# An attention and feed-forward kernel: the first feed-forward product of the last three token groups as seven block products, two of them with softplus in one pass, and another order from the middle on

## The chip, the core and the metric

The kernel runs on one core of a Trainium2 chip. Its time is the device time of one execution in microseconds (us); the three runs shown below are taken of the kernel as it stands before the change. The engines are TensorE (PE, matmuls; PEld is its weight load), VectorE (DVE), ScalarE (ACT), GpSimd (POOL), and SyncE (SP), whose queue issues nearly all transfers. Each engine works through its own list of instructions strictly in order and waits for the others by semaphores.

## What is computed

The attention output of 4 sequences of 768 tokens, 8 heads of 64 channels, is the input of a feed-forward layer with softplus between its two products:

```python
scores = scale * np.matmul(q, k.transpose(0, 1, 3, 2))      # 4 x 8 x 768 x 768
keep   = is_global | is_local                               # 8 global keys, 96 local ones
bias   = -slopes[:, None, None] * dist[None, :, :]
a      = softmax(where(keep, scores + bias, -1e9))
x      = matmul(a, v).transpose(0, 2, 1, 3).reshape(3072, 512)
h      = x @ w_in                                           # 3072 x 512 by 512 x 2048
g      = np.maximum(h, 0.0) + np.log1p(np.exp(-np.abs(h)))  # softplus
out    = g @ w_out                                          # 3072 x 2048 by 2048 x 512
```

## The kernel before

**Tiles.** The 3072 tokens are 24 blocks of 128 (numbered n in the order in which they are attended), two blocks make a unit of loading (i, 12 of them), and two make a token group (g, 12 of them, 256 tokens) for the feed-forward layer. Weights and activations are bf16 in SBUF; products accumulate in fp32 in PSUM.

**The order is written out by hand.** Every piece of work is an operation with a name, an engine and the tiles that it reads and writes (`Program.op`, L28). The string `ORDER` (L68) lists all names with a letter for the engine (P is PE, V is DVE, A is ACT, G is POOL, S is SP); `in_order` (L56) issues them in just this order, so each engine's list is the sequence of its own letters in the string. Waits follow from the tiles: a PSUM bank that is written again waits for whoever still reads it. Where an operation may run on several engines (`alts`), the letter decides.

**Names.** Attention of block n: `ldq`, `ldk`, `ldv` (loads of a unit), `castq`, `castk`, `castv` (to bf16), `trq`, `trk` (transposes on the DMA, issued by SP, L839 and L832), `gk`, `gv` (small copies of the global keys and values), `sc` (scores, L952, 16 matmuls into both halves of `s_ps`), `z` (DVE adds the bias, L978, two per block), `ex` (ACT Exp, L985, two per block), `pv` (probabilities by values, L1004, 8 matmuls of 65 columns, two per block, into the bank `x_ps`), `nm` (DVE reciprocal and multiply, L1015 and L1016), `xt` (transpose on the DMA into `XT`, L1047).

Feed-forward of group g: `a{g}.{p}`, p from 0 to 7 (L1062), is the first product: 8 matmuls of 128 x 128 weights by 256 columns, so 64 per group, alternating between the banks `h_ps0` and `h_ps1`. `e{g}.{p}` (ACT, L1077) takes Exp from PSUM to the tile `e`, and `ln{g}.{p//2}` (ACT, L1088) takes Ln of 1 plus that, which is the softplus, into the tile `g`, 128 x 1024 at a time. From group 2 on the second product is already done as seven block products instead of eight: `ka{g}.{j}` (L453, on DVE or POOL) forms five differences of 128 x 1024 bf16, `b{g}.{j}` (L523) is one block product of 8 matmuls of 256 columns, and `oe{g}.*` (L484 to L506) brings the sums from PSUM to the output tile `osb`. In groups 2 to 9 (`CHAIN`) all seven use the one bank `o_ps` in turn, with the order 3 4 1 5 2 7 6; each of `oe.a`, `oe.1`, `oe.c`, `oe.7` has to be read out before the bank is written again. Groups 10 and 11 use other banks, which are free by then (`S_KEYS`):

```python
CHAIN = range(FIRST_S, 10)
S_KEYS = {
    10: {"3": ("o",), "4": ("o",), "5": ("x",), "2": ("x",), "1": ("s", 0, 0), "7": ("s", 1, 0), "6": ("s", 1, 0)},
    11: {"3": ("o",), "4": ("o",), "5": ("x",), "2": ("x",), "1": ("s", 0, 0), "7": ("s", 1, 0), "6": ("h0",)},
}
```

Block numbers, products and second products are interleaved in the string, so that PE always has something to do while DVE and ACT read out what it wrote. The activation table is loaded once, at the start (`table`, L344); Exp and Ln are both in it.

## Time and profile before

| | |
|---|---|
| three timed runs | 210.65, 210.85, 211.04 us (median 210.85) |
| span of the profiled execution | 209.7 us, 5506 instructions |
| median less that span | 1.15 us |
| PE, PEld, DVE, ACT, POOL busy | 201.4, 164.7, 157.3, 174.1, 105.8 us |

The profiled execution is a fourth one, of which the page gives the span (first to last instruction on the core) and no total of its own; what lies around the span is therefore taken as the 1.15 us between it and the median. The granted TensorE clock is 1.000 throughout. In lists of instructions in order of time the columns are the start, the time until the last of the merged instructions ended, the engine, the line, the operation with its tiles, and how many were merged; a bracket gives the idle time before it and what ended it. A duration contains the way through the engine: consecutive instructions start closer together than their durations say, and that distance is what an instruction costs its engine.

### The profile page before, as it was taken

To read this page: it belongs to the slowest core of one execution; us is meant where nothing else is said; L and a number is where in the kernel's file an instruction comes from. 1 tells how busy PE (TensorE), PEld (TensorE's weight loads), DVE (VectorE), ACT (ScalarE), POOL (GpSimd) and SP (SyncE) were. 2 spreads that over 40 slices of the span, in tenths; PEclk is the share of its full clock that TensorE was granted. 3 is DMA by queue.
4 is the path that set the end of the run, shared out by engine and by line. 5 is a ranking of instruction groups with operands and counts; after the bars stand their busy time and mean duration, and the time that the engine had idled before them with its cause. 6 is when DMAs were issued, how large, how long until landed. Compare 5 with 4: busy or idle time off the path is not lost.

```text
span 209.7 us, 5506 instructions
## 1 busy us (share of the span) xinstructions
PE 201.4 (96%) x2202; PEld 164.7 (79%) x2211; DVE 157.3 (75%) x298; ACT 174.1 (83%) x253; POOL 105.8 (50%) x112
## 2 busy tenths in 40 slices
...
GB/s 181 363 363 389 387 354 350 330 222 278 174 308 201 237 193 279 223 205 194 256 152 266 164 191 238 100 104 194 208 100 3 50 5 125 128 0 0 103 91 109
DMA packets 70648, 40.98 MB, mean 195 GB/s; under 512 B 30432, under 2 KB 62688, under 8 KB 70624
## 3 DMA queue, kind: packets, MB, share of 16 engines
...
q10 hardware_dynamic: 688, 0.66, 0.9%
q8 instruction: 17, 0.28, 0.5%
q14 instruction: 7, 0.06, 0.2%
...
## 4 chain that ended last, share of the span: by engine, by line
PE 75%; DMA 13%; DVE 5%; SPq 3%; issue 1%; POOL 1%; ACTq 0%; ACT 0%; DVEq 0%
PE h_ps L1062 34%; PE o_ps L523 22%; DMA kT<-kb 6%; DMA raw<-in_moe_w_in_dram 5%; PE s_ps L952 5%; PE x_ps L1004 4%; PE s_ps L1109 3%; PE o_ps L1109 3%; DMA raw<-in_q_dram 3%; PE s_ps L523 1%; DVE z L978 1%; SPq L600 1%; PE x_ps L523 1%; SPq L1047 1%; SPq L1141 1%
## 5 line engine op out<-in xcount | busy, mean ns | idle before, releaser
L1062 PE MATMUL h_ps<-XT,w_in_bf 128*128 128x256 bf16 x768 | 95.2, 273 | 0.5 <-POOL w_in_bf L645 0.4
L1062 PEld LDWEIGHTS <-w_in_bf 128*128 128x128 bf16 x768 | 72.3, 98 | 11.2 <-POOL w_in_bf L645 0.6
L1077 ACT ACTIVATE e<-h_ps 128x512 f32<-128x512 f32 x96 | 59.4, 637 | 14.4 <-PE h_ps L1062 14.1
L1088 ACT ACTIVATE g<-e 128x1024 bf16<-128x1024 f32 x48 | 50.2, 1054 | 0.3
L978 DVE TENSOR_TENSOR z<-s_ps,biasA 128x1024 f32<-128x1024 f32 x38 | 45.8, 1217 | 3.5 <-PE s_ps L952 1.6
L453 POOL TENSOR_TENSOR g<-g 128x1024 bf16<-128x1024 bf16 x13 | 28.4, 2187 | 35.2 <-DVE raw L453 23.7
L985 ACT ACTIVATE pb<-z 128x1024 bf16<-128x1024 f32 (+1 forms) x44 | 43.3, 995 | 3.1 <-DVE z L978 2.5
L523 PEld LDWEIGHTS <-g 128*128 128x128 bf16 x320 | 31.1, 98 | 3.5
L523 PEld LDWEIGHTS <-raw 128*128 128x128 bf16 x240 | 22.9, 98 | 2.5
L523 PE MATMUL o_ps<-raw,raw 128*128 128x256 bf16 x192 | 24.2, 273 | 0.0
L453 DVE TENSOR_TENSOR raw<-g 128x1024 bf16<-128x1024 bf16 x23 | 16.2, 724 | 6.5 <-ACT g L1088 4.3
L870 POOL COPY vb<-vb 4x512 bf16<-4x512 bf16 x15 | 10.1, 672 | 21.1 <-PE x_ps L1004 20.8
L523 PE MATMUL o_ps<-raw,g 128*128 128x256 bf16 x160 | 20.1, 273 | 0.0
L1004 PEld LDWEIGHTS <-pb 128*128 128x128 bf16 x352 | 16.5, 98 | 3.8 <-ACT pb L985 0.4
L708 POOL CAST vb<-raw 64x512 bf16<-64x512 f32 x24 | 16.8, 700 | 5.0 <-DMA raw<-in_v_dram 3.9
L1016 DVE TENSOR_TENSOR xs<-x_ps,rcp 128x256 bf16<-128x256 f32 x40 | 17.0, 425 | 1.4
L453 POOL TENSOR_TENSOR raw<-g 128x1024 bf16<-128x1024 bf16 x7 | 14.9, 2126 | 3.9 <-PE o_ps L523 2.5
L1004 PE MATMUL x_ps<-vb,pb 128*128 128x65 bf16 x304 | 15.8, 193 | 0.0
L523 PE MATMUL o_ps<-w_out_bf,g 128*128 128x256 bf16 x128 | 15.8, 273 | 0.0
L1015 DVE RECIPROCAL rcp<-x_ps 128x4 f32<-128x4 f32 x40 | 7.1, 178 | 11.0 <-PE x_ps L1004 10.8
L1237 PE MATMUL x_ps<-blank 128*128 128x512 bf16 x33 | 11.4, 469 | 1.2 <-DVE blank L1161 1.2
L487 DVE TENSOR_TENSOR osb<-osb,o_ps 128x512 f32<-128x512 f32 x8 | 5.5, 687 | 8.9 <-PE o_ps L523 8.0
(119 smaller groups left out, 228.5 us busy)
## 6 DMA issues: line engine op xcount, KB each, us to landing
raw<-in_v_dram SPq DMA_DIRECT2D x12, 512.0 KB, 5.1
...
raw<-in_q_dram SPq DMA_DIRECT2D x9, 512.0 KB, 5.9
raw<-in_k_dram SPq DMA_DIRECT2D x9, 512.0 KB, 5.9
raw<-in_moe_w_in_dram SPq DMA_DIRECT2D x8, 512.0 KB, 9.4
raw<-in_moe_w_out_dram SPq DMA_DIRECT2D x8, 512.0 KB, 9.5
...
```

Of the source, the lines that this page charges most:

```text
L453: (nc.vector if eng == "DVE" else nc.gpsimd).tensor_tensor(dst, a[0], b[0], ALU.subtract)
L523: nc.tensor.matmul(psum(j), lhs[:, f // 2, f % 2, :], w(f), start=(f == 0 and not (chain and j in "267")), stop=(f == 7), skip_group_check ...
L708: copy_on[eng](dst, src)
L978: nc.vector.tensor_tensor(z, src, bias, ALU.add)
L985: nc.scalar.activation(pb[:, 0:nr, :].rearrange("p (y a) b -> p y (a b)", y=2), src, AF.Exp, scale=1.0 / root_d)
L1004: nc.tensor.matmul(xv[:, h, :], pb[:, 4 * (h % 2) + 2 * part + h // 2 if lone else u_all * (2 * (h % 2) + h // 2) + u, :], vb_of(prev if u ...
L1016: nc.vector.tensor_tensor(xs[:, 4 * part : 4 * part + 4, :], xv[:, :, 0:D], rcp[:][:, :, None].to_broadcast([P, 4, D]), ALU.mult,)
L1062: last = nc.tensor.matmul(hv[:, j, :], w_in_bf[:, m, fb * P : fb * P + P], XT[g % NXG][:, m, :], start=(m == 0), stop=(m == NM - 1),)
L1077: nc.scalar.activation(e[:, p % 2, :, :].rearrange("p j (b t r) -> p (j b) r t", b=2, r=2), hb[:].rearrange("p (a r t) -> p a r t", a=4, r=2),
L1088: nc.scalar.activation(gt[:, 2 * p - 2 : 2 * p + 2, :].rearrange("p a t -> p (a t)"), e[:].rearrange("p a j t -> p (a j t)"), AF.Ln, bias=1.0,
L1109: nc.tensor.matmul(bank(key)[:, 0 : z - a], gt[:, fb, ns * P : ns * P + P], w_out_bf[:, fb, a:z], start=(fb == 0), stop=(fb == NFB - 1),)
L1237: nc.tensor.matmul(x_ps[:], blank[:, 0:P], blank[:])
```

## The change

**First products of groups 9, 10 and 11** (`mm1_seven`). The 64 matmuls of 256 columns of a group become, for each of four slices i of the 2048 hidden channels, seven block products of 4 matmuls of 128 columns, 112 per group. They need sums and differences of weight blocks (`kw`, ten operations of 128 x 1024 bf16, made once) and of token blocks (`kx`, five per group, 128 x 256 bf16). The parts of a slice are a chain through one PSUM bank:

`mA` (product 1, 4 matmuls) - `my` (ACT or DVE copies it to a tile T) - `mB` (products 3 and 4) - `mt` (DVE adds both to T) - `mC` (5 and 2) - `eo` (ACT, first half of the result) - `mD` (7 and 6) - `md` (DVE: T less the bank) - `ed` (ACT, second half).

```diff
+            op(f"mA{g}.{i}", "PE", 0.22, r, part("1"), reads=needs("1"), writes=[xkey], after=first, count=4)
+            op(f"my{g}.{i}", "ACT", 0.4, r + 0.3, lambda eng, X=X, T=T: copy_on[eng](T, X[:, 0:W]), reads=[xkey], writes=[tk],
+               alts={"ACT": 0.4, "DVE": 0.42})
+            op(f"mB{g}.{i}", "PE", 0.45, r + 0.6, part("34"), reads=needs("34"), writes=[xkey], count=8)
+            op(f"mt{g}.{i}", "DVE", 0.75, r + 0.8, begin, reads=[xkey], writes=[tk], count=2)
+            op(f"mC{g}.{i}", "PE", 0.45, r + 1.0, part("52"), reads=needs("52"), writes=[xkey], count=8)
...
+            how = dict(table=SOFT_TABLE if soft else EXP_TABLE)
+            fn = AF.Softplus if soft else AF.Exp
+            op(f"eo{g}.{i}", "ACT", 0.64, r + 1.5, act(X, outs[0], fn), reads=[xkey], writes=ok[0], **how)
+            op(f"mD{g}.{i}", "PE", 0.45, r + 2.0, part("76"), reads=needs("76"), writes=[xkey], count=8)
+            op(f"md{g}.{i}", "DVE", 0.69, r + 2.5, end, reads=[xkey, tk], writes=[dk])
+            op(f"ed{g}.{i}", "ACT", 0.64, r + 3.2, act(D_, outs[1], fn), reads=[dk], writes=ok[1], **how)
+            if not soft:
+                op(f"ln{g}.{i}", "ACT", 0.99, r + 3.9, log, reads=ok[0] + ok[1], writes=gk[0] + gk[1], **how)
```

The matmuls of a part, and the two DVE operations of `mt` and the one of `md`:

```diff
+                        for f in range(2):
+                            for m in range(2):
+                                nc.tensor.matmul(
+                                    at[j][:, P * f : P * f + P], w[:, m, P * f : P * f + P], b[:, m, :],
+                                    start=f == m == 0 and j in "13", stop=m == 1, skip_group_check=True,
+                                )
...
+            def begin(X=X, T=T):
+                nc.vector.tensor_tensor(T, T, X[:, 0:W], ALU.add)
+                nc.vector.tensor_tensor(T, T, X[:, W:], ALU.add)
...
+                nc.vector.tensor_tensor(
+                    D_.rearrange("p (a c) -> p a c", a=2), T[:, None, :].to_broadcast([P, 2, W]),
+                    X.rearrange("p (a c) -> p a c", a=2), ALU.subtract,
+                )
...
+                op(f"kw{j}.{h}", "DVE", 0.0, rank, ex, reads=xk + yk, writes=[("WI", j, h)], port=True,
+                   after=users(("raw", slots[z], h)), alts={"DVE": 0.64, "POOL": 2.15})
...
+            op(f"kx{g}.{j}", "DVE", 0.0, rank, ex, reads=bk[a[1] : a[1] + 1] + bk[b[1] : b[1] + 1], writes=[key],
+               port=True, alts={"DVE": 0.25, "POOL": 0.6})
```

**Softplus in one pass.** Groups 10 and 11 take `AF.Softplus` straight from PSUM (or from D) into `g`, without `ln`. Its table is another one than that of Exp and Ln, and is loaded once, behind the last of these (`ln9.2`):

```diff
+EXP_TABLE, SOFT_TABLE = "natural_log_exp_and_others", "softplus"
+MM1S = (9, 10, 11)
+MM1_SOFT = (10, 11)
...
+        wants = [o for o in (self.ops[name] for name in self.placed) if o.table]
+        for o, p in zip(wants, wants[1:]):
+            if p.table != o.table:
+                o.then = p.table
...
         o.ins = o.fn()
+        if o.then:
+            table(o.then)
```

Group 9 has two banks for its chains (`h_ps0`, `h_ps1`), groups 10 and 11 four (also one half of each `s_ps`).

**Second products of groups 10 and 11.** Group 10 joins the chain on the one bank `o_ps`; group 11 gets banks of its own, and reads out 5, 2, 6 and 7 one by one (`sub_one`, `add_one`, 128 x 256 each):

```diff
-CHAIN = range(FIRST_S, 10)
+CHAIN = range(FIRST_S, 12)
+APART = (11,)
 S_KEYS = {
-    10: {"3": ("o",), "4": ("o",), "5": ("x",), "2": ("x",), "1": ("s", 0, 0), "7": ("s", 1, 0), "6": ("s", 1, 0)},
-    11: {"3": ("o",), "4": ("o",), "5": ("x",), "2": ("x",), "1": ("s", 0, 0), "7": ("s", 1, 0), "6": ("h0",)},
+    11: {"3": ("x",), "4": ("x",), "1": ("s", 0, 0), "5": ("o",), "7": ("o",), "2": ("s", 1, 0), "6": ("s", 1, 0)},
 }
```

**The order.** On PE, the first 120 names and their order are the same as before (to `b1.1.4`), and nearly so on the other engines. From there on the string is another: 75 operations change their engine among DVE, ACT and POOL, and the attention of the last blocks comes earlier (`sc23.0` stands before `b7.3` instead of after `b8.1`), since all Exp has to be done before the softplus table is loaded. The places of which the prediction speaks, as the string has them after the change (lines of the string in order, "..." where some are left out):

```
101: xt6:S b1.1.12:P ws3.4:V gv7.0:G e2.3:A sc8.0:P trq5:S ex7.1:A b1.1.14:P z8.1:V castk5.0:G pv7.0:P a2.5:P ln2.1:A
102: nm7.0:V trk5.0:S e2.5:A z8.0:V pv7.1:P castv4.01:G a2.4:P ex8.1:A nm7.1:V a2.7:P e2.4:A castv4.00:V xt7:S ex8.0:A
103: gk9:V a2.6:P castv4.11:V castv4.10:V e2.7:A ldv5:S pv8.0:P sc9.0:P e2.6:A nm8.0:V st0.0.0:S ln2.2:A ldk6:S oc1.1.0:V
104: pv8.1:P a3.1:P ldq6:S z9.0:V gv9.1:G ln2.3:A trk5.1:S a3.0:P gv9.0:G nm8.1:V ex9.0:A b2.3:P ka2.6:V xt8:S e3.1:A
...
118: e5.5:A gv14.0:G ka4.7:V b4.3:P st3.1.0:S castv9.10:A ka4.1:G st2.1.0:S ln5.2:A pv14.0:P trq8:S sc15.0:P nm14.0:V
119: e5.6:A a5.7:P z15.1:V ln5.1:A st3.0.0:S pv14.1:P a6.0:P ldk9:S e5.7:A gv15.1:V gv15.0:G z15.0:V ldq9:S b4.4:P
120: castv9.01:G e6.0:A trk8.1:S castv10.11:V ex15.1:A castv7.10:G a6.1:P nm14.1:V ka4.5:V kw1.1:G xt14:S a6.2:P gk16:A
121: ex15.0:A oe4.a:V sc16.0:P e6.1:A pv15.0:P z16.0:V b4.1:P e6.2:A castv8.10:A castv8.01:G a6.3:P nm15.0:V ln6.0:A
...
134: ex21.1:A z21.0:V st5.1.0:S pv20.1:P a8.6:P e8.5:A castv11.11:G trk11.1:S oe6.a:A ka7.6:V kx9.1:G a8.7:P e8.6:A
135: nm20.1:V st5.0.0:S gk22:A b6.1:P gv21.1:V castv11.01:G e8.7:A xt20:S gv21.0:V ex21.0:A mA9.0:P kx9.6:G oe6.1:V mA9.1:P
...
142: xt22:S ka8.6:V ed9.3:A mD9.2:P oe7.c:V ka8.2:G ln9.3:A mA10.2:P mA10.3:P md9.2:V pv23.0:P b7.7:P my10.2:V ed9.2:A
143: nm23.0:V mA10.0:P mA10.1:P my10.0:A mB10.2:P ka8.1:G ex23.1:A mB10.0:P mt10.2:V b7.6:P ln9.2:A mt10.0:V mC10.2:P
144: oe7.7:V mC10.0:P ka8.7:G pv23.1:P st7.1.0:S b8.3:P nm23.1:V st7.0.0:S eo10.0:A my10.1:V xt23:S b8.4:P kx10.6:V
145: eo10.2:A ka8.5:G mB10.1:P oe8.a:A mD10.0:P mt10.1:V b8.1:P md10.0:V mD10.2:P oe8.1:V my10.3:A mC10.1:P ed10.0:A
...
151: mD11.1:P oe9.7:V mB11.3:P md11.1:V st9.0.0:S b10.3:P ka10.7:V st9.1.0:S b10.4:P mt11.3:V mD11.2:P ka10.5:V oe10.a:A
152: mC11.3:P md11.2:V b10.1:P eo11.3:A ed11.2:A mD11.3:P oe10.1:V ed11.1:A md11.3:V b10.5:P ed11.3:A b10.2:P ka11.6:G
153: b11.3:P oe10.c:V b10.7:P b10.6:P ka11.2:V ka11.1:V b11.4:P ka11.7:V b11.1:P oe10.7:V oe11.a:A ka11.5:V st10.1.0:S
154: b11.2:P oe11.1:V st10.0.0:S b11.5:P oe11.2:V st11.1.0:S b11.6:P oe11.5:V b11.7:P oe11.6:V st11.1.1:S st11.0.1:S
155: oe11.7:V st11.0.0:A
```

Between `a5.0` and `b6.1` of the string stand, on DVE, before: 12 `z`, 12 `nm`, 9 `oe`, 11 `ka`, 4 casts and 5 small copies; after: 16 `z`, 17 `nm`, 10 `oe`, 11 `ka`, 6 `kw`, 7 casts, 4 small copies and 1 `kx`. On POOL, before: 4 `ka`, 7 casts and 4 small copies; after: 5 `ka`, 3 `kw`, 13 casts, 10 small copies and 1 `kx`. On PE, before: 24 `a`, 19 `b`, 12 `pv`, 6 `sc`; after: 32 `a`, 18 `b`, 17 `pv`, 8 `sc`.

Between the issue of a transpose by SP and the scores that read its result, the string after the change has on PE:

```
trk4.0  to sc8.0:  b1.1.4 b1.1.6 b1.1.8 pv6.1 sc7.0 a2.2 a2.3 b1.1.10 b1.1.12    (before: pv6.1 sc7.0 a2.2 a2.3 b1.1.6 b1.1.8 pv7.0)
trq6    to sc12.0: pv10.0 sc11.0 a4.1 pv10.1 a4.2 b2.7 b2.6 a4.3
trk7.0  to sc14.0: pv12.0 a4.7 b3.5 b3.2 a5.0 pv12.1 a5.1
trq8    to sc16.0: sc15.0 a5.7 pv14.1 a6.0 b4.4 a6.1 a6.2                        (before: pv14.0 a5.7 b4.1 pv14.1 a6.1 b4.5 b4.2 a6.3)
trq9    to sc18.0: a6.5 sc17.0 b4.7 pv16.0 a6.7 b4.6 a6.6
trk10.0 to sc20.0: b5.2 a7.7 a7.6 pv18.1 b5.7 b5.6 pv19.0
trq11   to sc22.0: a8.5 pv20.1 a8.6 a8.7 b6.1 mA9.0 mA9.1
```

In this list a `b1.1.x` is two matmuls of 512 columns; the products of groups 0 and 1 are not of the block kind. From `trq5` to `sc10.0` there were a3.1 b2.3 a3.2 b2.4 pv9.0 a3.3 a3.4 pv9.1 before, and there are 20 names after.

302 lines of the change are left out of this document (211 added, 91 removed).

## The prediction

> **What bounds the kernel now.** I read the busy time of the engines in four stretches first (columns: span, busy time and instructions of PE, PEld, DVE, ACT, POOL, granted clock, DMA share, GB/s), then what PE waited for from 26 to 206 us.
>
> ```profile
> 0.00:25.85 25.85, 22.29 (x218) 13.72 (x222) 19.07 (x54) 20.22 (x37) 13.05 (x24) 1.00 0.98 336
> 25.85:100.00 74.15, 72.55 (x811) 56.99 (x818) 61.95 (x106) 69.29 (x96) 47.85 (x54) 1.00 1.18 254
> 100.00:206.50 106.50, 106.50 (x1175) 93.96 (x1173) 75.75 (x139) 84.58 (x121) 44.92 (x34) 1.00 0.55 122
> 206.50:209.70 3.20, 0.02 (x1) 0.00 (x0) 0.48 (x2) 0.00 (x0) 0.00 (x0) 1.00 0.43 149
> ...
> PE s_ps L952 <- DMA kT<-kb: 1.2, 3, 0.7
> ...
> 65.05 0.62 PE L952 MATMUL s_ps<-qT,kT 64*128 64x128 bf16 x16 [0.17 <-DMA kT<-kb]
> ...
> 78.92 0.62 PE L952 MATMUL s_ps<-qT,kT 64*128 64x128 bf16 x16 [0.65 <-DMA kT<-kb]
> ...
> 98.05 0.23 PE L952 MATMUL s_ps<-qT,kT 64*128 64x128 bf16 x2 [0.36 <-DMA kT<-kb]
> ```
>
> PE bounds it: from 100 to 206.5 us it never stops, at full clock, while DVE is busy for 75.75 of 106.5 us (71%) and POOL for 42%. The last 3.2 us are one read-out and the last store. So whatever PE saves is saved at the end, but only as long as nothing makes PE wait; the present order has no such wait after 98 us. Those of `sc8.0`, `sc10.0` and `sc12.0` (0.17 + 0.65 + 0.36 = 1.18 us) are for transposes.
>
> **1. The matmuls: -2.2 us.**
>
> ```profile
> 153.32 1.91 PE L1062 MATMUL h_ps<-XT,w_in_bf 128*128 128x256 bf16 x16
> 155.07 0.41 PE L1004 MATMUL x_ps<-vb,pb 128*128 128x65 bf16 x8
> 155.31 1.04 PE L523 MATMUL o_ps<-raw,raw 128*128 128x256 bf16 x8
> ...
> 12.80 0.61 PE L812 MATMUL s_ps<-ident_p,qb 128*128 128x128 bf16 x8
> 13.24 0.29 PE L1004 MATMUL o_ps<-vb,pb 128*128 128x65 bf16 x4
> ...
> L812 PE MATMUL s_ps<-ident_p,qb x16: 219/219/219, 12.8 to 22.6; 128*128 128x128 bf16 x16
> ...
> 22.15 0.54 PEld L812 LDWEIGHTS <-qb 128*128 128x128 bf16 x8
> ```
>
> Sixteen 256-column matmuls hold PE for 155.07 - 153.32 = 1.75 us: 0.109 us each, 0.87 for an `a` or `b`. The nearest to the new ones are the transposes on PE, 128 columns with a new 128 x 128 weight for each: (0.61 - 0.219)/7 = 0.056 us (0.44 us from start to start for eight). 192 x 0.109 = 20.95 us go, 3 x 112 x 0.056 = 18.78 come: -2.17. Below, exactly half a column time gives 336 x 0.0546, -2.6; above, the slowest row, weights loaded every (0.54 - 0.098)/7 = 0.063 us (0.098 being one load), +0.2. I take the matmul row, since matmuls of 65 columns with full weights run closer still (0.24 us for eight).
>
> **2. Read-outs that PE now waits for: +1.4 us.**
>
> ```profile
> 164.56 1.91 PE L523 MATMUL o_ps<-raw,g 128*128 128x256 bf16 x16
> 166.30 1.04 PE L1062 MATMUL h_ps<-XT,w_in_bf 128*128 128x256 bf16 x8
> ...
> 166.50 0.69 DVE L484 COPY osb<-o_ps 128x512 f32<-128x512 f32 x1 [1.20 <-PE o_ps L523]
> ...
> 24.75 1.05 POOL w_in_bf L645
> 25.85 1.05 PE h_ps L1062 x8
> ...
> 162.25 0.62 PE L952 MATMUL s_ps<-qT,kT 64*128 64x128 bf16 x16
> 162.80 1.92 PE L1062 MATMUL h_ps<-XT,w_in_bf 128*128 128x256 bf16 x16
> ...
> 162.96 2.35 DVE L978 TENSOR_TENSOR z<-s_ps,biasA 128x1024 f32<-128x1024 f32 x2
> ...
> 173.25 0.17 DVE L1015 RECIPROCAL rcp<-x_ps 128x4 f32<-128x4 f32 x1
> 173.46 0.42 DVE L1016 TENSOR_TENSOR xs<-x_ps,rcp 128x256 bf16<-128x256 f32 x1
> ```
>
> PE to DVE takes 0.20 us from the start of PE's next work (166.50 - 166.30), another engine's end to PE 0.05. A read-out of 128x512 (0.69) therefore needs 0.94 us of other PE work between the product and the next write of its bank, `nm` (0.21 + 0.42) needs 0.88. What the string puts there: between `b10.1` and `b10.5` only `mD11.3`, 0.45: PE waits 0.49. Between `pv8.0` and `pv8.1` only `sc9.0`, 0.55: 0.33. Before `pv7.1`, `nm7.0` stands behind `z8.1` on DVE, so from the end of `sc8.0` it takes 0.20 + 1.13 + 0.63 + 0.05 = 2.01 against b1.1.14 (1024 columns at the pace above, 0.44), pv7.0 (0.24) and a2.5 (0.87): 0.46. Ahead of `b9.7`, `b10.3` and `b10.7` 0.15 together. Sum 1.43. In the chains, `mB` needs 0.7, `mC` 1.0 and `mD` 0.9 us of cover, and nearly all have it: `mD11.3` stands behind `mC11.3` and `b10.1`, 0.87 against 0.89. If a row is shorter by 0.1 at each of the seven places, 0.8 remains; nothing lets it become a gain.
>
> **3. Transposes: -1.2 and +1.2 us.**
>
> ```profile
> L839 SPq DMA_TRANSPOSE qT<-qb x9: 1231/1259/2601, 39.8 to 151.0; - x9
> ...
> DMA to landing us min/median/max: 3.0/4.9/6.4
> ...
> L832 SPq DMA_TRANSPOSE kT<-kb x14: 1194/1247/2343, 43.1 to 141.8; - x14
> ...
> DMA to landing us min/median/max: 2.6/4.4/6.5
> ...
> raw<-in_q_dram SPq DMA_DIRECT2D x9, 512.0 KB, 5.9
> ```
>
> At the three old waits the PE work between transpose and scores was 3.6, 5.7 and 4.2 us; the new string gives them 4.7 (`trk4.0`), over 10 and 5.4, so I drop all 1.18. But it leaves less ahead of others: 4.6 us for `trk7.0`, 4.7 for `trk10.0`, 5.2 each for `trq8` and `trq9`, 5.4 for `trq6`, 4.2 for `trq11`. At the median landings only `trq11` is short; at the maxima the q transposes lack 1.2, 1.2, 1.0 and 2.2. Midway, 5.65, three of them lack 0.5 + 0.5 + 0.2; `trq11` runs late, when 3.0 was seen. Sum +1.2, bounds 0 and 5. The loads themselves I price at nothing: `ldv9` to `ldv11` move ahead by 7 to 23 us of PE's work, the DMA share of 0.55 after 100 us leaves room for them, and the last one, `ldq11`, keeps 7.7 us of PE's work until its cast against 5.9 to land. If that cover were short, `castq11`, `trq11` and `sc22.0` would be late by the difference.
>
> **4. DVE and POOL: +1.2 us.**
>
> ```profile
> 120.14 2.30 POOL L453 TENSOR_TENSOR g<-g 128x1024 bf16<-128x1024 bf16 x1 [1.36 <-DVE raw L453]
> ...
> 121.41 1.57 DVE L453 TENSOR_TENSOR raw<-g 128x1024 bf16<-128x1024 bf16 x1
> ...
> L453 DVE TENSOR_TENSOR raw<-g 128x1024 bf16<-128x1024 bf16 x23 | 16.2, 724 | 6.5 <-ACT g L1088 4.3
> ...
> L453 DVE TENSOR_TENSOR g<-g 128x1024 bf16<-128x1024 bf16 x7 | 4.8, 688 | 0.0
> ...
> L708 DVE CAST vb<-raw 64x512 bf16<-64x512 f32 x13 | 5.8, 446 | 0.7 <-DMA raw<-in_v_dram 0.4
> L494 DVE TENSOR_TENSOR osb<-osb,s_ps 128x512 f32<-128x512 f32 x2 | 1.4, 684 | 0.1
> L490 DVE TENSOR_TENSOR osb<-osb,x_ps 128x256 f32<-128x256 f32 x2 | 0.8, 422 | 1.8 <-issue 1.7 <-PE x_ps L523 0.2
> ```
>
> The chains give DVE 12 `mt` (two of 0.42 each), 12 `md` (0.68), five `my`, six `kw` (0.69), four `kx`: some 21 us at 0.08 less per instruction back to back. Between `a5.0` and `b6.1`, DVE's names cost 35.0 us before, against 43.3 of PE (24 + 19 at 0.87, the rest `pv` and `sc`); afterwards 47.7 against 51.5. The margin falls from 19% to 7%, and POOL's share rises from 15.7 of 43.3 (36%) to 31.1 of 51.5 (60%). In the rows above a bf16 sum on DVE that starts while POOL is in one of its own takes 1.57 us instead of 0.69. Of the 30 such DVE sums that one did (it alone lifts the mean of 23 to 724 ns); chance at POOL's 42% would have given about 12. At the same ratio 29 DVE operations of this kind with POOL at 60% meet 1.5 times: 1.3 us of lateness, of which I let 0.9 reach PE. The queue ahead of `oe4.a` (z15.1, gv15.1, z15.0, a cast of 0.45, nm14.1, ka4.5; the small gv15.1 taken as another 0.4) takes 5.1 us from `sc15.0`, against 5.4 of PE until `b4.1`; if `nm14.0` (0.55), which stands first, is late too, PE waits: +0.3. So 0.9 + 0.3. Bounds: 0, and +4 if the meetings follow chance (17 of 0.9 us, of which a quarter reaches PE).
>
> The Trainium skill (SBUF - State Buffer, "SBUF: two separate sides") says that POOL and DVE hold their shared ports as an exclusive lock for a whole instruction, the loser blocked fully. The 1.57 agrees; by that rule the last bound is the likely case wherever this order slips.
>
> **5. ACT: 0.**
>
> ```profile
> L1077 ACT ACTIVATE e<-h_ps 128x512 f32<-128x512 f32 x96 | 59.4, 637 | 14.4 <-PE h_ps L1062 14.1
> L1088 ACT ACTIVATE g<-e 128x1024 bf16<-128x1024 f32 x48 | 50.2, 1054 | 0.3
> L345 ACT ACT_TABLE_LOAD x1 | 1.3, 1283 | 1.5 <-PEq L1374 1.5
> ```
>
> Eight `ln` (1.05 each) go, seven `my` come: ACT gets lighter behind `ln9.2`, and was not the bound. No row has Softplus; Exp and Ln differ only with size here, so I price it as `e` (0.64); 0.1 more would show at `mD11.3` alone. The second table load (1.28) is covered: from `mD9.2`, md, ed, my10.0, ex23.1, ln9.2, the load and eo10.0 take 5.6 us, PE has 7.1 of other work ahead of `mD10.0`. Uncovered it would cost its 1.28.
>
> The Trainium skill (ScalarE: Activation LUTs, "What ACT_TABLE_LOAD costs") puts a switch at 2.66 us with the drain ahead of it. By that `oe8.a`, queued behind, would be late and `b8.1` wait some 0.4 us; no row here shows a drain.
>
> **Sum.** -2.17 + 1.43 - 1.18 + 1.2 + 1.2 = +0.48 us on the span of 209.7: 210.2, with the 1.15 around it 211.3. Up to `b1.1.4` (some 50 us) nothing changes, because the names stand in the same order; behind the last product the read-out (128x256) and the store are as before.
>
> **Rivals.** *A, faster:* PE waits only where part 2 is certain. 210.85 - 2.17 - 1.18 + 1.43 gives 208.9. For it speaks that the old order, with the same kinds of cover, shows no wait in 106 us; against it the 7% margin. *B, slower by 1.5%:* POOL and DVE meet as chance has it, +4 instead of +1.2: 211.3 + 2.8 = 214.1. POOL's new 60% and DVE's 93% speak for it, against it that the order keeps the two apart as the old one did. It decides from the point at which DVE, in `a5.0` to `b6.1`, falls behind by more than its 3.8 us. *C, no saving at all:* the 128-column matmuls run at the pace of the weight rows, +0.2 for -2.17: 213.7; the matmul rows speak against it.
>
> **Chances.** Forecast 0.42 (own range 210.3 to 212.4), A 0.30, B 0.22, C 0.06. No change means within 0.2%, 0.42 us, about what a measurement here can tell. Faster: 0.28 of A and 0.03; same: 0.02 of A and 0.15; slower: 0.24 of the forecast with B and C, 0.52. The range reaches from A's lower part to B: 208.5 to 214.3.
>
> **What would show it.** Eight-matmul `m` parts 0.45 us apart: part 1. PE idle ahead of `b10.5`, `pv7.1`, `pv8.1`, released by DVE: part 2. PE waiting for qT or kT in front of `sc16.0` and `sc18.0`, and no longer of `sc10.0`: part 3. DVE or POOL sums of 128x1024 well over their 0.69 and 2.3, and DVE above 90% from 115 to 155 us: part 4. The forecast is wrong if PE again never waits after 100 us (A), or if it waits over 6 us there (B).

## The result, and the profile after

The changed kernel takes 217.76 us (median of four runs, 217.03 to 218.62), the kernel before 210.94 us (median of four, 210.65 to 211.35) beside it: a ratio of 1.0331, interval 1.0297 to 1.0365. So it is 3.3% slower, and the forecast of 211.3 us is 6.5 us too low and outside its range. The profiled execution took 218.16 us.

The page's head and busy times of the changed kernel, then its windows (the columns are those of the windows of before):

```profile
span 216.1 us, 5880 instructions
...
PE 202.8 (94%) x2347; PEld 165.6 (77%) x2355; DVE 183.3 (85%) x349; ACT 168.2 (78%) x247; POOL 129.8 (60%) x130
...
100.00:206.50 106.50, 102.43 (x1281) 90.90 (x1278) 92.67 (x168) 79.94 (x118) 71.27 (x63) 0.98 0.54 118
...
60.00:100.00 40.00, 38.09 (x464) 32.41 (x462) 36.65 (x72) 36.26 (x51) 18.68 (x16) 1.00 1.08 218
100.00:135.00 35.00, 31.43 (x361) 26.38 (x357) 31.18 (x51) 27.32 (x40) 22.27 (x25) 0.95 0.93 200
```

The same two stretches of the kernel before:

```profile
60.00:100.00 40.00, 38.77 (x466) 33.32 (x466) 32.52 (x58) 37.23 (x53) 21.96 (x26) 1.00 1.19 227
100.00:135.00 35.00, 35.00 (x418) 30.71 (x417) 29.41 (x55) 32.59 (x48) 16.35 (x16) 1.00 0.96 198
```

PE has 13.3 us without work (216.1 - 202.8), before it had 8.3. From 100 to 135 us it stops for 3.6 us, where before it never did, and its clock falls to 0.95. DVE's share from 60 to 100 us rises from 81% to 92%. What PE waits for now (us in total, times, longest):

```profile
PE x_ps L1035 <- DVE xs L1047: 3.2, 5, 1.2
...
PE o_ps L547 <- DVE osb L502: 1.1, 1, 1.1
PE h_ps L1230 <- DMA XT<-xs: 0.7, 1, 0.7
```

The three waits for kT are gone; five for `nm`, one for `oe4.a` and one for a transposed group have come, and two small ones (0.4 and 0.3 us) for other read-outs. The costliest place, in order of time:

```profile
111.04 2.13 POOL L1108 TENSOR_TENSOR raw<-w_in_bf 128x1024 bf16<-128x1024 bf16 x1
...
111.72 1.73 DVE L739 CAST vb<-raw 64x512 bf16<-64x512 f32 x1
...
113.70 0.42 DVE L1047 TENSOR_TENSOR xs<-x_ps,rcp 128x256 bf16<-128x256 f32 x1
...
114.05 1.09 DVE L471 TENSOR_TENSOR g<-g 128x1024 bf16<-128x1024 bf16 x1
...
114.28 0.40 PE L1035 MATMUL x_ps<-vb,pb 128*128 128x65 bf16 x8 [1.22 <-DVE xs L1047]
...
115.06 0.68 DVE L502 COPY osb<-o_ps 128x512 f32<-128x512 f32 x1
...
115.79 1.56 PE L547 MATMUL o_ps<-raw,raw 128*128 128x256 bf16 x8 [1.11 <-DVE osb L502]
...
117.14 3.09 PE L1230 MATMUL h_ps<-XT,w_in_bf 128*128 128x256 bf16 x16
```

Read it from the top. POOL starts `kw1.1`. DVE's next cast, `castv10.11`, takes 1.73 us (other casts of its size take 0.43) and ends 0.28 us behind POOL's sum. Behind it on DVE stand `nm14.1`, `ka4.5` (itself stretched, 1.09 instead of 0.68) and `oe4.a`, all late; `pv15.0` waits 1.22 us for the first, `b4.1` 1.11 us for the last. Then PE itself is slow: eight matmuls of 256 columns took 117.14 - 115.79 = 1.35 us instead of 0.87, the next sixteen took 2.93 (the row after them starts at 120.07) instead of 1.75. The windows of these microseconds say why; the number behind POOL's share is the clock (0.57, 0.50, 0.50):

```profile
116.00:117.00 1.00, 1.00 (x8) 0.73 (x6) 0.97 (x3) 0.47 (x1) 0.62 (x3) 0.57 1.25 199
117.00:118.00 1.00, 1.00 (x7) 0.69 (x6) 1.00 (x3) 0.00 (x0) 0.00 (x0) 0.50 0.57 97
118.00:119.00 1.00, 1.00 (x6) 0.75 (x5) 1.00 (x2) 0.00 (x0) 0.00 (x0) 0.50 0.35 55
```

After 2.33 us of waiting, PE ran at half clock, which cost 0.48 + 1.18 = 1.66 us more. The place cost 4.0 us in all. Not all of that is due to `kw1.1`: without it (e3 below) 1.06 us of the two waits remain.

The second costliest place is of the same kind, with a cast of POOL in the sum's place. DVE's sum `ka5.6` takes 1.47 us instead of 0.68, `nm17.0` stands behind it, and `pv17.1` waits 1.04 us:

```profile
130.76 1.03 POOL L707 CAST qb<-raw 128x1024 bf16<-128x1024 f32 x1
130.87 1.47 DVE L471 TENSOR_TENSOR raw<-g 128x1024 bf16<-128x1024 bf16 x1
...
132.94 0.40 PE L1035 MATMUL x_ps<-vb,pb 128*128 128x65 bf16 x8 [1.04 <-DVE xs L1047]
```

### The profile page after: what moved, and what is told of

The parts are those of the page before. It is cut to its first block, busy times and chain, and to the rows that moved or that the text cites. A ratio compares the mean times of both kernels' runs of the same rounds, so it can differ in the third digit from the quotient of the medians.

```text
span 216.1 us, 5880 instructions
## 1 busy us (share of the span) xinstructions
PE 202.8 (94%) x2347; PEld 165.6 (77%) x2355; DVE 183.3 (85%) x349; ACT 168.2 (78%) x247; POOL 129.8 (60%) x130
## 4 chain that ended last, share of the span: by engine, by line
PE 69%; DVE 13%; DMA 10%; ACT 3%; issue 2%; SPq 1%; POOL 1%; ACTq 0%; DVEq 0%
PE h_ps L1230 23%; PE o_ps L547 22%; PE h_ps L1170 6%; DMA raw<-in_moe_w_in_dram 4%; PE x_ps L1035 4%; DVE z L1009 4%; PE s_ps L983 4%; PE s_ps L1289 3%; DMA raw<-in_q_dram 3%; PE o_ps L1289 3%; DMA XT<-xs 2%; PE s_ps L1170 2%; DVE raw L471 1%; PE s_ps L547 1%; DVE xs L1047 1%
## 5 line engine op out<-in xcount | busy, mean ns | idle before, releaser
L1230 PE MATMUL h_ps<-XT,w_in_bf 128*128 128x256 bf16 x576 | 72.1, 276 | 1.1 <-DMA XT<-xs 0.7
L1230 PEld LDWEIGHTS <-w_in_bf 128*128 128x128 bf16 x576 | 54.9, 99 | 9.8 <-issue 1.3
L1258 ACT ACTIVATE e<-h_ps 128x512 f32<-128x512 f32 x72 | 44.3, 636 | 10.8 <-PE h_ps L1230 10.6
L1268 ACT ACTIVATE g<-e 128x1024 bf16<-128x1024 f32 x36 | 37.3, 1054 | 0.4
L471 POOL TENSOR_TENSOR raw<-g 128x1024 bf16<-128x1024 bf16 x12 | 25.7, 2143 | 16.5 <-ACT g L1182 8.2
L547 PE MATMUL o_ps<-raw,raw 128*128 128x256 bf16 x224 | 28.9, 276 | 1.1 <-DVE osb L502 1.1
L739 POOL CAST vb<-raw 64x512 bf16<-64x512 f32 x26 | 20.2, 780 | 13.1 <-DMA raw<-in_v_dram 12.2
L547 PEld LDWEIGHTS <-raw 128*128 128x128 bf16 x240 | 22.7, 98 | 4.3 <-issue 1.2
L471 POOL TENSOR_TENSOR g<-g 128x1024 bf16<-128x1024 bf16 x9 | 19.7, 2192 | 7.3 <-DVE raw L471 6.9
L547 PE MATMUL o_ps<-raw,g 128*128 128x256 bf16 x144 | 17.5, 272 | 0.0
L1170 PEld LDWEIGHTS <-raw 128*128 128x128 bf16 x240 | 14.9, 98 | 0.9 <-DVE e L1196 0.4
```

What stands on the lines that cost most here:

```text
L471: (nc.vector if eng == "DVE" else nc.gpsimd).tensor_tensor(dst, a[0], b[0], ALU.subtract)
L547: nc.tensor.matmul(psum(j), lhs[:, f // 2, f % 2, :], w(f), start=(f == 0 and not (chain and j in ("67" if g in APART else "267"))), stop= ...
L739: copy_on[eng](dst, src)
L1170: nc.tensor.matmul(at[j][:, P * f : P * f + P], w[:, m, P * f : P * f + P], b[:, m, :], start=f == m == 0 and j in "13", stop=m == 1, skip ...
L1230: last = nc.tensor.matmul(hv[:, j, :], w_in_bf[:, m, fb * P : fb * P + P], XT[g % NXG][:, m, :], start=(m == 0), stop=(m == NM - 1),)
L1258: nc.scalar.activation(e[:, p % 2, :, :].rearrange("p j (b t r) -> p (j b) r t", b=2, r=2), hb[:].rearrange("p (a r t) -> p a r t", a=4, r=2),
```

## The experiments

The theory after the first look, M: the loss sits in the middle of the new order, where read-outs come late on DVE; part of it are meetings, that is, operations of POOL and DVE that run at the same time and make DVE's one longer. The rivals: P, the new products and their sums are to blame; D or F, DVE has too much to do, whatever POOL does (against it L: the meetings count, not the load). "kw1.1 moved" is the third experiment below and the base of most others. Ratios are against the kernel before, run on the same chip.

| run | median us | ratio | interval |
|---|---|---|---|
| changed kernel | 217.76 | 1.0331 | 1.0297 to 1.0365 |
| e1 old middle, new products | 230.57 | 1.0916 | 1.0867 to 1.0965 |
| e2 new middle, old products | 217.92 | 1.0306 | 1.0264 to 1.0349 |
| e3 kw1.1 later | 215.17 | 1.0180 | 1.0144 to 1.0216 |
| e4 fillers in the two waits | 216.80 | 1.0249 | 1.0203 to 1.0296 |
| e5 POOL's ka short | 214.30 | 1.0150 | 1.0110 to 1.0189 |
| e6 five places mended | 215.42 | 1.0196 | 1.0157 to 1.0235 |
| e7 order alone | 215.37 | 1.0186 | 1.0144 to 1.0229 |
| e8 before, scores later | 211.56 | 1.0030 | 1.0001 to 1.0060 |
| e9 eleven back from DVE | 220.70 | 1.0454 | 1.0397 to 1.0512 |
| e10 DVE's ka short | 216.43 | 1.0240 | 1.0196 to 1.0283 |
| e11 nine sums to DVE | 217.55 | 1.0298 | 1.0272 to 1.0324 |
| e12 ka4.1 to DVE | 215.19 | 1.0159 | 1.0120 to 1.0199 |
| e13 no long POOL sums | 213.70 | 1.0102 | 1.0068 to 1.0136 |
| e14 that, and DVE lighter | 214.33 | 1.0138 | 1.0088 to 1.0188 |
| e15 three sums to DVE | 214.07 | 1.0113 | 1.0064 to 1.0163 |
| e16 nm7 first | 213.02 | 1.0085 | 1.0053 to 1.0116 |
| e17 read-outs first | 214.04 | 1.0132 | 1.0103 to 1.0161 |

### The middle against the products (e1, e2, e7)

For e1 the string before up to `a5.4` and near it up to `sc20.0`, then the changed one; for e2 the other way round; e7 is e2 with everything from `a10.6` on in the order of before.

All three differ in most lines of the string; around `b4.1` (the changed string first, then e1) and around `a10.6` (e2 first, then e7) they read:

```diff
-gk16:A ex15.0:A oe4.a:V sc16.0:P e6.1:A pv15.0:P z16.0:V b4.1:P e6.2:A castv8.10:A castv8.01:G a6.3:P
+z15.0:V nm14.1:V castv8.00:A castv9.00:A ka4.5:V ka4.2:V b4.1:P a6.0:P e5.7:A a6.1:P gk16:A e6.0:A
...
-nm23.1:V e10.5:A b9.4:P ln10.1:A ka9.1:G a10.6:P oe9.a:V e10.6:A a10.7:P xt23:S b9.1:P
+ka9.2:G a10.7:P st8.1.0:S e10.7:A a10.6:P oe9.a:A a11.1:P e10.6:A b9.1:P e11.1:A a11.0:P
```

> The changed kernel's products (seven block products in groups 9 to 11, softplus in one pass), but with the order of the kernel before up to a5.4 name for name and close to it up to the scores of block 20; the weight sums kw are spread behind that. Theory M (the loss sits in the changed order of the middle, 50 to 150 us, where DVE's read-outs come late): the PE waits for xs and osb between 50 and 150 us vanish, the clock stays at 1.00, and the saved columns are left over: 208.5 to 211. Rival P (the loss belongs to the new products: their sums on DVE and POOL and their chains): still 214 to 218.

> The kernel before in all that is computed, but with the changed kernel's order up to the start of group 9's first product (its kw and kx left out because there are none), then the old products. Theory M: the same waits as in the changed kernel (pv15.0 and b4.1 near 114 us, pv7.1 near 62 us), 213 to 217. Rival P: without the new sums nothing is late, 210.5 to 212.

> As the new middle with the old products, but the last part (from a10.6 on) in the exact order of the kernel before, so that the read-outs behind the last product are those of before. Theory M: the middle's order alone costs 3.5 to 4.5 us, 214.5 to 216. Rival P: 211 to 213, the 217.9 of the first try having been a matter of its last read-outs.

e1 fails as an experiment: my own order made new waits, so it says nothing on the products. It shows the mechanism at its plainest, though. Two DVE operations in a row met POOL's sums (normal 0.68 and 0.36 us), and the copy that PE waited for stood behind them:

```profile
194.68 2.59 DVE L471 TENSOR_TENSOR g<-g 128x1024 bf16<-128x1024 bf16 x1 [1.52 <-POOL raw L471]
...
197.20 2.20 DVE L1134 TENSOR_TENSOR kb<-XT 128x256 bf16<-128x256 bf16 x1
199.32 0.41 DVE L1205 COPY e<-h_ps 128x256 f32<-128x256 f32 x1
...
199.78 0.48 PE L1170 MATMUL h_ps<-qb,w_in_bf 128*128 128x128 bf16 x3 [4.17 <-DVE e L1205]
```

e2 came out above M's range. PE's last work began at 209.62 there and the span ended at 216.6, so some of its loss lay in its last read-outs; e7 mends that. Its 1.9% belongs to the order alone, with the old products and no `kw` and `kx` at all. Its waits are the ones of the changed kernel, smaller:

```profile
PE x_ps L1004 <- DVE xs L1016: 1.2, 4, 0.6
...
PE o_ps L523 <- DVE osb L484: 0.7, 1, 0.7
```

Rival P falls for 1.9 of the 3.3%. Most of the rest hangs on the place of `kw1.1` (next part), which is one of the new products' own sums; so much is left of P.

### kw1.1's place, and the clock (e3, e4)

```diff
-castv10.11:V ex15.1:A castv7.10:G a6.1:P nm14.1:V ka4.5:V kw1.1:G xt14:S a6.2:P
+castv10.11:V ex15.1:A castv7.10:G a6.1:P nm14.1:V ka4.5:V xt14:S a6.2:P
...
-e6.4:A trq9:S a6.5:P gk17:G gv16.0:V
+e6.4:A trq9:S a6.5:P gk17:G kw1.1:G gv16.0:V
```

> The changed kernel with one name moved: the weight sum kw1.1 on POOL (2.13 us at 111.0 us, in front of DVE's cast of 1.73 us) goes behind gk17, into 5.7 us in which POOL is idle. Theory M with port meetings: the cast takes its 0.43 us, pv15.0 and b4.1 no longer wait (1.22 and 1.11 us), the clock is not halved behind them (some 1.7 us): 213.5 to 215.5. Rival D (DVE is merely full, POOL has nothing to do with it): the waits stay or come back a few names later, 216.5 to 218.

One name moved gives back 1.5% (1.0331 to 1.0180, 3.2 us). The same place in e3:

```profile
109.89 1.95 POOL L739 CAST vb<-raw 64x512 bf16<-64x512 f32 x3
...
111.27 0.86 DVE L739 CAST vb<-raw 64x512 bf16<-64x512 f32 x1
...
112.72 0.68 DVE L471 TENSOR_TENSOR g<-g 128x1024 bf16<-128x1024 bf16 x1
...
112.95 0.40 PE L1035 MATMUL x_ps<-vb,pb 128*128 128x65 bf16 x8 [0.35 <-ACT e L1258]
...
114.06 1.03 PE L547 MATMUL o_ps<-raw,raw 128*128 128x256 bf16 x8 [0.71 <-DVE osb L502]
...
116.20 1.22 DVE L1009 TENSOR_TENSOR z<-s_ps,biasA 128x1024 f32<-128x1024 f32 x1
116.23 2.12 POOL L1108 TENSOR_TENSOR raw<-w_in_bf 128x1024 bf16<-128x1024 bf16 x1
...
117.33 1.57 DVE L707 CAST qb<-raw 128x1024 bf16<-128x1024 f32 x1
```

The waits of 1.22 and 1.11 us are now 0.35 and 0.71, not gone as expected, and the clock isn't halved here. The cast still takes 0.86 us: it ends 0.29 us behind casts of POOL (109.89 + 1.95 = 111.84). DVE's two stretched operations are shorter by 0.87 and 0.41 us than in the changed kernel, 1.28 together, and PE's two waits by 1.27: here the whole of a lateness on DVE reaches PE. Part of the gain is not `kw1.1`'s own: the cast of POOL that met `ka5.6` comes too late for that here, and `pv17.1` waits 0.25 us instead of 1.04.

The bias sum beside `kw1.1`, which reads PSUM, takes its normal 1.22; the cast behind it, from SBUF to SBUF, is held until the sum ends (1.57 instead of 0.68). So the new place isn't free either; this comes back in e10.

```diff
+        if (g, p) in ((6, 3), (6, 4)): op(f"y{g}.{p}", "PE", 0.875, rank, fn, count=8, reads=..., writes=[hkey])
...
-sc16.0:P e6.1:A pv15.0:P z16.0:V b4.1:P e6.2:A
+sc16.0:P e6.1:A y6.3:P pv15.0:P z16.0:V e6.2:A y6.4:P b4.1:P
```

> The changed kernel with two products done twice: a6.3 once more ahead of pv15.0, a6.4 once more ahead of b4.1, 0.87 us of needless PE work each, put into the two waits. Theory C (PE idle for most of 2.7 us is what halves its clock for 3.4 us): the clock stays at 1.00, the two waits are filled but not shortened, and the kernel gets faster by 1.2 to 1.8 us, 216 to 216.6. Rival (the halved clock comes at its own times, or costs nothing on the path): 217.5 to 218.5.

0.8% faster (1.0331 to 1.0249) with 1.75 us of needless work added, a little less than theory C expected; its interval ends where that of the changed kernel begins. Only the first wait was filled. The second product was done in time, and PE still waited for `oe4.a`:

```profile
115.97 1.03 PE L547 MATMUL o_ps<-raw,raw 128*128 128x256 bf16 x8 [1.27 <-DVE osb L502]
```

`b4.1` starts as late as in the changed kernel, at 115.97 against 115.79, but what follows runs at full pace (1.75 us for sixteen, 116.84 to 118.59), and the clock is 0.998 to 1.000 in all six executions. In the changed kernel it was 0.990 in two of four (spans 216.1 and 216.6), 0.997 and 0.998 in the others (215.3 and 214.9). So the halving isn't certain without the fillers either: if they did nothing, two halved executions among ten would both fall to the changed kernel about once in eight times. That the fillers keep the clock fits, but isn't shown.

### Load or meetings (e5, e9, e10, e11, e12)

In order e5, e10 (a token sum on the engine named works on 64 columns; in e10 those of groups 4 to 6, since DVE has none of the sums named for group 3), e9, e11 and e12, all on e3:

```diff
-tensor_tensor(dst, a[0], b[0], ALU.subtract)
+tensor_tensor(*((x if eng == "DVE" or g < 4 else x[:, :, :, 0:8]) for x in (dst, a[0], b[0])), ALU.subtract)
...
+tensor_tensor(*((x[:, :, :, 0:8] if eng == "DVE" and g in (3, 4, 5, 6) and j in ("3452" if g == 3 else "12567") else x) for x in (dst, a[0], b[0])), ALU.subtract)
...
-gk9:V oe2.a:V oe3.a:V oe4.a:V castv8.11:V castv4.00:V castv4.10:V castv5.11:V castv5.00:V ka2.7:V ka2.2:V
+gk9:A oe2.a:A oe3.a:A oe4.a:A castv8.11:A castv4.00:G castv4.10:G castv5.11:G castv5.00:G ka2.7:G ka2.2:G
...
-ka2.5:G ka3.7:G ka3.5:G ka3.2:G ka4.6:G ka4.1:G kw1.1:G kw1.0:G ka5.1:G
+ka2.5:V ka3.7:V ka3.5:V ka3.2:V ka4.6:V ka4.1:V kw1.1:V kw1.0:V ka5.1:V
...
-castv8.00:V e5.5:A gv14.0:G ka4.7:V b4.3:P st3.1.0:S castv9.10:A ka4.1:G
+castv8.00:V e5.5:A gv14.0:G ka4.1:V ka4.7:V b4.3:P st3.1.0:S castv9.10:A
```

> The kernel with kw1.1 moved, and in it POOL's token sums ka of groups 4 and later work on 64 of their 1024 columns only (the other columns are left out, so the second product's operands are not formed there); DVE's list is untouched. Theory L (DVE loses its time beside POOL's sums): DVE's lengthened operations get fewer, the PE waits for xs and osb between 100 and 135 us shrink by half or more, 213 to 214.5 against 215.2 for kw1.1 moved alone. Rival D (DVE is full by its own list, POOL plays no part beyond kw1.1): within 0.5 of 215.2.

> The kernel with kw1.1 moved, and in it eleven operations that the change had brought to DVE run again where they ran before, each at its place in the string: gk9, oe2.a, oe3.a, oe4.a and castv8.11 on ACT, castv4.00, castv4.10, castv5.11, castv5.00, ka2.7 and ka2.2 on POOL. DVE gets some 5.7 us lighter between 55 and 115 us. Theory F (DVE is full there, 91 to 98% of each 10 us, and PE's waits are what DVE cannot do in time): DVE falls to 88% or less, 213 to 214.3 against 215.2. Rival K (no engine has room: ACT and POOL come late in DVE's stead, or POOL's added sums stretch DVE's operations): 215 to 216.5.

> The kernel with kw1.1 moved, and in it DVE's ten token sums ka of groups 4 to 6 work on 64 of their 1024 columns only (the rest of these operands is left out); POOL's list is untouched. DVE gets some 6 us lighter between 100 and 150 us. Theory F (DVE is full): the PE waits for xs and osb between 105 and 135 us vanish (2 us in the trace of kw1.1 moved), 212.8 to 213.8. Theory L (not the load but the meetings with POOL count): the waits shrink by less than half, 214.5 to 215.5.

> The kernel with kw1.1 moved, and in it the nine long sums that POOL does between 75 and 124 us (ka2.5, ka3.7, ka3.5, ka3.2, ka4.6, ka4.1, kw1.1, kw1.0, ka5.1; 2.1 to 2.5 us each) done by DVE, each at the point of DVE's list where POOL had begun it. Nothing else is changed. DVE takes on 9 x 0.62 = 5.6 us, POOL loses 20 us. Theory L (each meeting of a POOL sum with a DVE operation that reads and writes SBUF alone costs DVE more than the sum itself): no worse than kw1.1 moved, 213.5 to 215.2, with DVE's lengthened operations in that stretch gone. Theory F (DVE's load is what counts): PE waits for 4 us or more in addition, 217 to 220.

> The kernel with kw1.1 moved, and in it one POOL sum, ka4.1 (2.12 us from 104.55, beside which DVE's cast castv8.00 took 1.93 instead of 0.43), done by DVE right behind that cast. DVE takes on 0.62 us there and should be rid of 1.5. Theory L: the waits at b4.7's and pv14.1's places (0.17 and 0.19 us in that trace) vanish and those of pv15.0 and b4.1 shrink, 214.2 to 215. Theory F: 215.2 to 216.

e5's time is where L expects it, but its interval overlaps that of e3, and in its trace PE stops for 1.9 us between 100 and 135 us (2.0 in e3's), where L wanted half; alone it settles nothing. (`kw1.1` is still on POOL there, and `castq9.0` took 2.31 us beside it.) e10 goes against the load: with some 6 us less to do on DVE the kernel isn't faster, in the medians it is slower (1.0240 against 1.0180; the intervals overlap), above both forecasts. The slower part needn't be its doing: in its trace PE waited 1.45 us for `XT` at 67.97, ahead of anything that e10 changes. Between 100 and 135 us PE stops for 1.9 us, against 2.0 in e3's. There a new wait stands in the place of the old ones (1.62 us):

```profile
117.87 2.12 POOL L1108 TENSOR_TENSOR raw<-w_in_bf 128x1024 bf16<-128x1024 bf16 x1
118.15 2.40 DVE L707 CAST qb<-raw 128x1024 bf16<-128x1024 f32 x1 [0.81 <-DMA raw<-in_q_dram]
...
121.81 0.92 PE L547 MATMUL o_ps<-raw,raw 128*128 128x256 bf16 x7 [1.62 <-DVE osb L521]
```

DVE was early, and even idle for 0.81 us; its cast `castq9.0` then met nearly the whole of `kw1.1`. In e12 `castv8.00` was rid of its meeting (0.42 instead of 1.93), and `castq9.0` met `kw1.1` in the same way (2.44), so nothing was gained. In e9 DVE was lighter too, and the kernel slower by 2.7%, far above both forecasts: POOL's added sums came late themselves (PE waited 1.43 and 1.68 us for them), and a cast beside one took 1.96.

e11 speaks for the load: nine sums moved to DVE cost 1.2%. Its worst new wait shows how. `ka2.5` now stands ahead of a bias sum, the Exp waits for that, and PE for the Exp's engine:

```profile
77.47 0.68 DVE L471 TENSOR_TENSOR g<-g 128x1024 bf16<-128x1024 bf16 x1
...
78.07 1.21 DVE L1009 TENSOR_TENSOR z<-s_ps,biasA 128x1024 f32<-128x1024 f32 x1
...
79.31 1.06 ACT L1016 ACTIVATE pb<-z 128x1024 bf16<-128x1024 f32 x1 [0.62 <-DVE z L1009]
...
80.96 1.03 PE L1230 MATMUL h_ps<-XT,w_in_bf 128*128 128x256 bf16 x8 [1.46 <-ACT e L1258]
```

So neither count alone sets the time. What decides is what stands ahead of each read-out on DVE, and how long that takes; a meeting is the dearest thing that can stand there.

### Without meetings (e13, e14, e15)

The moves common to all three, on the changed kernel; e13 has e5's short sums besides, e14 those of e5 and e10, and e15 has none of them but e12's move:

```diff
-nm14.1:V ka4.5:V kw1.1:G xt14:S
+nm14.1:V ka4.5:V xt14:S
...
-castk9.0:G z16.1:V b4.5:P
+castk9.0:G z16.1:V kw1.1:V b4.5:P
...
-gk17:G gv16.0:V ex16.0:A gv16.1:G oe4.c:V sc17.0:P nm15.1:V kw1.0:G
+gk17:G gv16.0:V kw1.0:V ex16.0:A gv16.1:G oe4.c:V sc17.0:P nm15.1:V
```

> The changed kernel with kw1.1 and kw1.0 done by DVE (behind z16.1 and gv16.0), and POOL's token sums ka of groups 4 and later on 64 of their 1024 columns only (the rest of these operands is left out). So POOL has no long sum between 93 and 135 us, and DVE does 1.3 us more than with kw1.1 moved. Theory L (meetings): DVE's casts castv8.00 and castq9.0 take 0.43 and 0.7 us, PE waits for less than 1.2 us between 100 and 135 us, 212.5 to 214. Theory F (DVE's load): the waits there stay at 2 us or more, 214.5 to 216.

> As the one without long POOL sums, and DVE's token sums ka of groups 4 to 6 short too (64 of 1024 columns): DVE is 6 us lighter between 100 and 150 us, with no long POOL sum there. Theory L: no change against the one without long POOL sums (within 0.5). Theory F: its remaining waits between 100 and 135 us go, 1 us or more less; if both hold, this is the fastest of the changed order, 211.5 to 213.

> The changed kernel with three of POOL's sums done by DVE and nothing left out: kw1.1 (behind z16.1), kw1.0 (behind gv16.0) and ka4.1 (behind castv8.00). DVE takes on 1.9 us and is rid of the meetings of castv8.00 (1.5 us) and castq9.0 (0.9 us) with them. Theory L: 213.5 to 214.8. Theory F: 215.2 to 216.5, since DVE's load grows as in the nine sums.

The times are as theory L says. With POOL's long sums gone from that stretch the ratio falls to 1.0102 (the waits between 100 and 135 us are 1.3 us in that trace, just over the forecast), clear of e3's interval; taking 6 us of load from DVE on top gains nothing on the clock (1.0138, the intervals overlap). That doesn't clear the load altogether: in e14's trace PE stops for only 0.55 us between 100 and 135 us, but waits 1.47 us for `XT` at 67.69, ahead of anything that sets e14 apart. e15 computes all that the changed kernel does and is 2.1% faster than it. Where e3, e10 and e12 had casts of 1.57 to 2.44, it has:

```profile
118.55 0.68 DVE L1108 TENSOR_TENSOR raw<-w_in_bf 128x1024 bf16<-128x1024 bf16 x1
...
119.15 0.69 DVE L707 CAST qb<-raw 128x1024 bf16<-128x1024 f32 x1
...
121.66 1.03 PE L547 MATMUL o_ps<-raw,raw 128*128 128x256 bf16 x8 [0.18 <-DVE osb L521]
```

Against e3 the gain of e15 rests on the medians alone, and their intervals overlap. The trace, of the slowest of its six executions, shows 1.9 us of stops between 100 and 135 us, against 2.0 in e3's: other waits (0.58, 0.46 and 0.44 us for `osb`) stand where the old ones were.

### The read-outs themselves (e6, e16, e17), and the old waits (e8)

e6 (on e3), e16 (on e15), what e17 adds, and e8 (on the kernel before); only the names that change places, and what they pass:

```diff
-pv7.1:P a2.4:P | ka4.7:V nm14.0:V z15.1:V z15.0:V | castv10.11:V nm14.1:V ka4.5:V oe4.a:V
+a2.4:P pv7.1:P | nm14.0:V z15.1:V z15.0:V ka4.7:V | nm14.1:V castv10.11:V oe4.a:V ka4.5:V
-pv15.0:P b4.1:P a6.3:P a6.4:P | ka5.6:V nm17.0:V | ka5.5:V oe5.a:V
+a6.3:P pv15.0:P a6.4:P b4.1:P | nm17.0:V ka5.6:V | oe5.a:V ka5.5:V
...
-z8.1:V nm7.0:V z8.0:V nm7.1:V
+nm7.0:V z8.1:V nm7.1:V z8.0:V
...
-nm13.1:V oe3.7:V | ka4.7:V nm14.0:V z15.1:V | castv10.11:V nm14.1:V ka4.5:V oe4.a:V | ka5.6:V nm17.0:V | ka5.5:V oe5.a:V
+oe3.7:V nm13.1:V | nm14.0:V z15.1:V ka4.7:V | nm14.1:V castv10.11:V oe4.a:V ka4.5:V | nm17.0:V ka5.6:V | oe5.a:V ka5.5:V
...
-sc8.0:P a2.5:P | sc10.0:P a3.5:P | sc12.0:P a4.4:P
+a2.5:P sc8.0:P | a3.5:P sc10.0:P | a4.4:P sc12.0:P
```

> The kernel with kw1.1 moved, and five places at which its trace still shows PE waiting mended by order alone: a2.4 ahead of pv7.1; nm14.0 ahead of ka4.7; nm14.1 ahead of castv10.11 and oe4.a ahead of ka4.5; a6.3 ahead of pv15.0 and a6.4 ahead of b4.1; nm17.0 ahead of ka5.6 and oe5.a ahead of ka5.5. Nothing is computed otherwise. Theory M (what is left of the loss are these waits, 2.9 us in that trace): 211.5 to 213. Rival (the waits belong to a DVE that has too much to do and come back some names later): 214 to 215.5.

> The version with three of POOL's sums on DVE, and one more change of DVE's order near 61 us: nm7.0 ahead of z8.1 and nm7.1 ahead of z8.0 (both read-outs stood behind a bias sum of 1.21 us, so that pv7.1 waited and the transpose xt7 went out late; a3.1 waited 1.4 us for its XT). Nothing is left out. If these two waits are lost time (0.8 and 1.4 us in that trace): 212 to 213.3. If the later z8.0 is what pv8.0 then waits for, or XT lands no earlier: 213.5 to 214.5.

> As nm7 first, and five more read-outs put ahead of work that nobody waits for yet: oe3.7 ahead of nm13.1, nm14.0 and z15.1 ahead of ka4.7, nm14.1 ahead of castv10.11, oe4.a ahead of ka4.5, nm17.0 ahead of ka5.6 and oe5.a ahead of ka5.5. Nothing is left out. If PE's waits between 105 and 134 us (2.3 us) go with them: 210.5 to 212, as fast as the kernel before or faster. If DVE's list is merely shifted and the waits come back at its later names, as with the five places mended: 212 to 214.

> The kernel before with sc8.0, sc10.0 and sc12.0, which wait for kT there (1.18 us together), each put behind the next product on PE (a2.5, a3.5, a4.4). If these waits are lost time: 209.5 to 210.5 against 211.0 to 211.5. If the scores' own followers then run late: 211 to 212.5.

e6 gained nothing: the waits went from the places named and came back, 0.78 and 0.42 us for `osb` near 116 and 120 us, and 1.59 us for `XT` at 67.6. The last one has a chain of its own, which e15 shows:

```profile
63.77 1.19 SPq L1078 DMA_TRANSPOSE XT<-xs  x1
...
66.20 0.40 PE L1035 MATMUL x_ps<-vb,pb 128*128 128x65 bf16 x8 [0.18 <-DVE xs L1047]
...
68.02 1.92 PE L1230 MATMUL h_ps<-XT,w_in_bf 128*128 128x256 bf16 x16 [1.41 <-DMA XT<-xs]
```

`nm7.1` is late, so `xt7` goes out late, and `a3.1` needs it 2.8 us later. In this trace it landed 4.2 us after its issue. That isn't fixed: up to this point e3 and e13 do the same as e15, and there `xt7` landed after 2.8 and 2.5 us and PE waited for it by at most 0.2 us. So this wait comes and goes from one execution to the next by over 1 us, which blurs every comparison here of single traces. To put PE's products closer (e6) can't help; to put `nm7.0` and `nm7.1` ahead of the bias sums (e16) sends `xt7` out 0.9 us earlier: `pv7.1` no longer waits, nor does `a3.1`, but in that trace `xt7` also landed after 2.5 us. A new wait, 0.58 us for ACT at 64.0, takes part of it back. The gain over e15 is 1 us in the medians, with overlapping intervals. e17 takes it back: with DVE's order changed at six more places, PE waits 1.08 us near 108.8. e16 is the best of the changed order, 2.4% faster than the changed kernel and still 0.9% slower than the kernel before. No version beat that.

e8 shows that the old waits for kT weren't worth what the trace had put on them: two came back, 0.33 us for `XT` and 0.62 for kT at `sc12.0`, and the time didn't fall.

## Why the prediction was wrong

The sign was right, but a forecast of +0.2%, with a chance of 0.52 on slower, earns little for it. The mechanism of rival B (meetings on DVE and POOL reach PE) was right; its size, its count of meetings and its place in the odds were not.

**1. Matmuls: the pace right, the saving not.** Parts of eight start 0.45 us apart, as forecast:

```profile
200.22 0.61 PE L1170 MATMUL s_ps<-kb,raw 128*128 128x128 bf16 x8
200.67 0.61 PE L1170 MATMUL s_ps<-XT,raw 128*128 128x128 bf16 x8
201.11 1.04 PE L547 MATMUL o_ps<-raw,raw 128*128 128x256 bf16 x8
201.99 0.61 PE L1170 MATMUL s_ps<-kb,raw 128*128 128x128 bf16 x8
202.98 1.91 PE L547 MATMUL o_ps<-w_out_bf,g 128*128 128x256 bf16 x16 [0.39 <-DVE osb L505]
```

Added up from start to start over all rows of the changed kernel, the 336 matmuls and the waits right behind them hold PE for 20.0 us, against 20.95 (192 x 0.109 is 20.93) for the 192 that went: some 0.9 us saved where the prediction has 2.17. In the times it doesn't show: e3 and e7 differ in the products, and their ratios are 1.0180 and 1.0186, each to within 0.4%. Rival C (no saving by a slow pace) is wrong in its reason.

**2. Read-outs: right, as far as it went.** `pv7.1` waited 0.62 us (forecast 0.46), `pv8.1` 0.18 (0.33), `b10.5` 0.39 (0.49).

**3. Transposes: wrong both ways.** No wait for qT or kT came, so the +1.2 wasn't there. Whether the -1.18 was a gain is doubtful too, since in e8 it was none. And the transposes of `XT`, which I hadn't costed, are the ones that ran short: 0.7 us here, up to 1.6 in the experiments.

**4. DVE and POOL: the step that failed.** It was priced at +1.2 with a bound of +4. It named the right place, the queue ahead of `oe4.a`, and gave it 0.3 us; it cost 4.0. Two assumptions failed.

The first is the lateness: 1.5 meetings and 1.3 us were forecast, and between 94 and 145 us the trace has five operations of DVE that are stretched by 0.3 to 1.5 us, 4.3 us together (rival B had 17 of 0.9; they were fewer and dearer). The second is the share that reaches PE, 0.9 of 1.3 in the sum and a quarter in the bound. DVE works in order, so everything behind the stretched operation is late by the whole of it, and between e3 and the changed kernel 1.28 us on DVE were 1.27 on PE. PE's waits for `nm` and `oe4.a` between 100 and 135 us come to 3.6 us, and the half clock came on top.

In the runs that one place is worth 1.5% (e3 against the changed kernel) and the order alone 1.9% (e7). Of e3's 1.8%, the meetings that e15 takes out are 0.7%, the two bias sums ahead of `nm7` 0.3% (neither difference clears its interval; e13, without all long sums, clears e3's), and 0.9% remains in e16, where the trace still shows PE waits; I haven't taken those apart, so their cause stays open.

The rule of the Trainium skill quoted there (SBUF - State Buffer, "SBUF: two separate sides"), an exclusive lock for a whole instruction, agrees: the casts of 1.73 and 2.40 us end 0.3 and 0.6 us behind POOL's sum, and the bias sum, which reads PSUM, passes beside it. Had I taken the bound as the case, the forecast would have been 214.1, still 3.7 us too low.

**5. ACT: right.** The second table load took 1.28 us, and PE waited for none of it. Softplus, priced at 0.64, took 0.60 us from PSUM and 0.75 from SBUF, as Exp did. No drain of ACT showed: `ln9.2` ends at 176.58, the load runs from 176.59, and the next activation starts at 177.88. So the 2.66 us that the Trainium skill (ScalarE: Activation LUTs, "What ACT_TABLE_LOAD costs") gives for a switch isn't seen here.

**Missed altogether: the clock.** I took 1.00 as given. 1.66 us of the profiled execution were lost to it, and two of the four executions had a clock as low.
